# A third of the heads from head 10 on in key layout, exponentials kept in PSUM, in an LSH attention with a spatial gating MLP

## The chip, the cores and the metric

The program runs on one core of one Trainium2 chip. The metric is the device time of one execution in microseconds; of several executions, the median. A core has TensorE (PE; its weight loads are shown as PEld), VectorE (DVE), ScalarE (ACT), GpSimd (POOL) and the queue engine SyncE (SP), and sixteen DMA engines that all queues share.

## What is computed

Attention over 4 batches of 8 heads, 768 positions, head size 64, in which a query sees only the keys with the same 6-bit hash, followed by an MLP with a gate over positions. Cut to what matters:

```python
# q, k, v: (4, 8, 768, 64)
q_bits = (einsum('bhsd,dk->bhsk', q, proj) > 0)
k_bits = (einsum('bhsd,dk->bhsk', k, proj) > 0)
mask = q_bucket[:, :, :, None] == k_bucket[:, :, None, :]
scores = where(mask, scale * matmul(q, k.transpose(0, 1, 3, 2)), -1e9)
attn = exp(scores - max(scores, axis=-1))
attn = attn / (sum(attn, axis=-1) + 1e-09)
x = matmul(attn, v)                       # heads side by side: (4, 768, 512)

h = maximum(x @ w_in, 0.0)                # (4, 768, 1024)
u, w = h[..., :512], h[..., 512:]
w_n = (w - mean(w)) / sqrt(var(w) + 1e-06)
w_s = einsum('ts,bsd->btd', w_spatial, w_n) + b_spatial[None, :, None]
out = (u * w_s) @ w_out
```

## The kernel before

Numbers that need more than 16 bits are carried as two f16 tiles, a high and a low half, and a product of two such numbers takes three matmuls. The hash is folded into the score product: `ab[n % 4]` (four tiles in SBUF) holds queries, keys and hash rows of head n, so that scores and mask come out of four matmuls of 384 columns for each tile of 128 rows. There are 32 heads, n = 0 to 31, and 6 tiles each; two heads make a pair.

A head runs in one of two ways.

*Query layout* (`scores`, L278; `weighted`, L303). A tile has 128 queries in the partitions and 768 keys in the row. Four matmuls (L291, L292) fill a score buffer `sp`; VectorE finds the negated row maximum (L293, tile `jk`, value `nb`); ScalarE takes the exponential with that bias (L295) into an f32 tile `ex` in SBUF, of which there are three; ScalarE casts it to f16 as the high half of `pp` (L298); the low half is `ex` minus the high half (L299). That subtraction is on VectorE, but on GpSimd for tile 2 of the heads from 16 on, and for tiles 0 and 3 of the earlier ones (`PL_POOL`, `PL_POOL1`). Since the weighted sum needs keys in the partitions, a DMA turns `pp` into `pt` (L301, queue SP): 128 x 1536 f16. Then 18 matmuls (L314 to L316) add the tile to `pv`.

*Key layout* (`scores_k`, L256; `weighted_k`, L268), in heads 1 to 7, the set `KEYS`. A tile has 128 keys in the partitions, so that nothing has to be turned. But a row maximum over keys cannot be taken there, and it is found ahead: `row_max` (L235) makes two matmuls of 384 columns for each of six tiles (L241), a reduction on VectorE (L243), and after the sixth puts the maxima into a row of `ab` by way of a small transpose on PE and a transfer of `mt` on SP (L248 to L254). Scores then have the maximum subtracted already. The exponential (L265) goes to SBUF as f32, and six f32 matmuls (L275) weight `vf`, an f32 copy of v.

`normalize` (L318) divides `pv` by the row sums, `transpose_x` turns each pair's result by DMA (`xt`), and when a batch's four pairs are there its MLP is cut into 28 units (`mlp_units`: v, u, s and o), which are spread over the tiles of the next batch. The last batch's MLP runs after the last head. Weights are loaded, split and scaled in pieces during heads 0 to 12 (`weights_gen`).

*Buffers in PSUM.* The pool `ps_sc` has two score buffers of two banks each; `sp` of both layouts and the row maxima's `mp` take turns in them. Two banks are for `pv`, two for everything else. The pool is full.

*What sets the order.* The loop (L504) goes over g = 6 n + i. With `at(g, k)` each piece gets a due time: scores at g, the weighted sum of a query tile 5 tiles later (`LAG`), of a key tile 3 later (`LAGK`), the row maxima of head n from g = 6 n - 10 on, that is from the third tile of head n - 2. `build(n + 2)`, the loads of `ab`, is placed at tile 0 of head n, and after its transpose in SP's queue where head n is in query layout (L525). A scheduler then orders each engine's instructions by due time and by when it expects operands and buffers to be free; each engine executes its list strictly in order.

## Time and profile before

| | us |
|---|---|
| median of 3 runs | 736.97 |
| lowest, highest | 735.91, 740.86 |
| profiled execution, first to last instruction | 741.7 |
| one transpose of `pp`, time in SP's queue, median | 1.605 |
| score matmul of 384 columns (L291), mean | 0.344 |
| the 576 matmuls of the spatial product (L417), busy | 100.9 |

The profiled execution took 4.7 us more than the median of the runs. A group of matmuls overlaps itself: L417's 576 have a mean of 329 ns, but are busy for only 100.9 us together. Durations on PE are thus latencies, and the pace of a dense stretch is read from starts in the timeline. On the other engines an instruction's last 0.08 us or so can overlap the next one's start.

### The profile page before, as it was taken

The page shows a single profiled execution, that of the slowest core. Times are in us where ns is not written, and L with a number is a line of the kernel's source. Part 1 is how long each engine was busy: PE and PEld are TensorE (multiplying, and loading weights), DVE is VectorE, ACT ScalarE, POOL GpSimd, SP SyncE. Part 2 cuts the span into 40 slices and gives each one's busy share as a digit, 9 for nine tenths or more (in the row PEclk, how much of TensorE's full clock was granted, in tenths as well). Part 3 has the DMA queues.
Part 4 walks back from the last instruction along what each step waited for, and adds up shares of the span by engine and source line. Part 5 has one row for each costly group of instructions (what it writes and reads, how often), then busy time and mean ns, then how long its engine had stood idle before and what let it go on. Part 6 is the DMA issues. An engine that isn't in the chain of part 4 may idle for free.

```text
span 741.7 us, 14927 instructions
## 1 busy us (share of the span) xinstructions
PE 631.5 (85%) x5759; PEld 400.4 (54%) x5759; DVE 520.6 (70%) x945; ACT 434.8 (59%) x668; POOL 321.2 (43%) x324
## 2 busy tenths in 40 slices
PE   1569898998988776997898899889898998999997
PEld 0237686776445444554544555556455565654553
DVE  4677795536799999567689798678698987755200
ACT  1344574346788676655676577667677776743221
POOL 5122443123458675264314565156235571451503
PEclk9768797999999989898999999999999999999999
DMA  9565554324999989996999799999999999860011
GB/s 235 149 123 155 133 148 102 99 55 97 224 237 197 215 207 187 213 178 138 234 202 199 138 210 213 211 211 212 206 210 181 194 175 213 182 136 15 1 42 43
DMA packets 290011, 120.95 MB, mean 163 GB/s; under 512 B 270740, under 2 KB 273812, under 8 KB 289940
## 3 DMA queue, kind: packets, MB, share of 16 engines
q1 hardware_dynamic: 287636, 119.11, 76.4%
q10 hardware_dynamic: 2304, 0.89, 0.5%
q8 instruction: 45, 0.74, 0.4%
q14 instruction: 26, 0.21, 0.1%
HBM read 28.33 MB, written 6.29 MB: 47 GB/s over the span
## 4 chain that ended last, share of the span: by engine, by line
PE 43%; DMA 21%; DVE 13%; issue 8%; ACT 6%; POOL 6%; SPq 3%; ACTq 0%; DVEq 0%; POOLq 0%
DMA pt<-pp 14%; PE pv L275 6%; PE vps L361 6%; PE ops L432 5%; PE sps L417 5%; PE ups L402 5%; DMA ab<-hl 4%; PE sp L291 3%; DVE jk L293 3%; PE sp L292 3%; DVE pp L299 2%; PE sp L262 2%; PE pv L314 2%; ACT ex L295 2%; PE sp L263 2%
## 5 line engine op out<-in xcount | busy, mean ns | idle before, releaser
L295 ACT ACTIVATE ex<-sp,nb 128x768 f32<-128x768 f32 x150 | 134.1, 897 | 54.8 <-DVE jk L293 48.9
L299 DVE TENSOR_TENSOR pp<-ex,pp 128x768 f16<-128x768 f32 x116 | 126.2, 1089 | 47.6 <-ACT pp L298 46.5
L293 DVE TENSOR_SCALAR_CACHE_REDUCE jk<-sp 128x768 bf16<-128x768 f32 x150 | 142.4, 949 | 24.1 <-PE sp L292 22.2
L298 ACT CAST pp<-ex 128x768 f16<-128x768 f32 x150 | 124.3, 829 | 50.0 <-DMA pt<-pp 43.9
L314 PE MATMUL pv<-vp,pt 128*128 128x65 f16 x900 | 108.2, 198 | 40.5 <-DMA pt<-pp 40.2
L291 PE MATMUL sp<-ab 128*128 128x384 f16 x300 | 103.2, 344 | 31.6 <-ACT ex L295 19.3
L314 PEld LDWEIGHTS <-pt 128*128 128x128 f16 x900 | 86.7, 101 | 67.2 <-DMA pt<-pp 53.4
L299 POOL TENSOR_TENSOR pp<-ex,pp 128x768 f16<-128x768 f32 x34 | 58.1, 1708 | 131.1 <-ACT pp L298 124.6
L315 PE MATMUL pv<-vp,pt 128*128 128x64 f16 x900 | 108.0, 197 | 0.0
L316 PE MATMUL pv<-vp,pt 128*128 128x65 f16 x900 | 107.8, 198 | 0.0
L292 PE MATMUL sp<-ab 127*128 127x384 f16 x300 | 103.9, 346 | 0.0
L417 PE MATMUL sps<-ws,vn 128*128 128x384 f16 x576 | 100.9, 329 | 1.5 <-DVE sg L180 1.0
L315 PEld LDWEIGHTS <-pt 128*128 128x128 f16 x900 | 87.0, 100 | 11.3 <-issue 1.3
L316 PEld LDWEIGHTS <-pt 128*128 128x128 f16 x900 | 86.9, 100 | 3.1 <-issue 0.5
L417 PEld LDWEIGHTS <-vn 128*128 128x128 f16 x576 | 55.3, 99 | 37.8 <-issue 3.9
L432 PE MATMUL ops<-wo,g 128*128 128x512 f16 x288 | 70.9, 391 | 1.5 <-ACT o L436 0.9
L275 PEld LDWEIGHTS pv<-vf,ex 128*128 128x128 f32 x504 | 68.5, 208 | 4.1 <-issue 1.6
L402 PE MATMUL ups<-xt,wi 128*128 128x384 f16 x384 | 69.1, 333 | 1.3 <-ACT u L405 0.9
L361 PE MATMUL vps<-wi,xt 128*128 128x512 f16 x288 | 68.0, 383 | 1.4 <-DMA xt<-xs 1.3
L275 PE MATMUL pv<-vf,ex 128*128 128x65 f32 x504 | 67.0, 286 | 0.0
L333 POOL TENSOR_TENSOR x<-x,xf 128x384 f32<-128x384 f32 x32 | 35.5, 1110 | 64.1 <-DVE x L332 64.1
L422 POOL TENSOR_TENSOR sy<-sy,u 128x384 f32<-128x384 f32 x32 | 36.6, 1145 | 49.3 <-DVE sy L421 49.2
(87 smaller groups left out, 1010.7 us busy)
## 6 DMA issues: line engine op xcount, KB each, us to landing
qk<-kq SPq DMA_DIRECT2D x16, 768.0 KB
ab<-hl SPq DMA_DIRECT2D x31, 384.0 KB
ab<-hl SPq DMA_DIRECT2D x34, 192.0 KB
out<-o SPq DMA_DIRECT2D x24, 256.0 KB
v<-v SPq DMA_DIRECT2D x13, 384.0 KB
raw<-w_in SPq DMA_DIRECT2D x16, 256.0 KB
pt<-pp SPq DMA_TRANSPOSE x150
raw<-w_sp SPq DMA_DIRECT2D x12, 192.0 KB
```

Of the source, the lines that this page charges most:

```text
L275: nc.tensor.matmul(acc[:, qi, :], lhsT=ex[:, qi * P:(qi + 1) * P], rhs=vf[p % 2][:, 2 * i + e, :], start=(i == 0 and qi == 0), stop=(i == ...
L291: nc.tensor.matmul(ps[:, c], lhsT=t[:, 0, qs], rhs=t[:, 1, cs], start=True, stop=False)
L292: nc.tensor.matmul(ps[:, c], lhsT=t[0:P - 1, 3, qs], rhs=t[0:P - 1, 2, cs], start=False, stop=True)
L293: nc.vector.tensor_scalar(jk, ps, -ISQ, None, op0=ALU.mult, op1=ALU.min, accum_out=nb)
L295: st["ex", n, i] = nc.scalar.activation(ex, ps, AF.Exp, bias=nb, scale=ISQ).ins
L298: nc.scalar.copy(pp[:, 0], ex)
L299: (nc.gpsimd if i in (PL_POOL if n >= 2 * NH else PL_POOL1) else nc.vector).tensor_tensor(out=pp[:, 1], in0=ex, in1=pp[:, 0], op=ALU.subtract)
L314: nc.tensor.matmul(acc, lhsT=pt[:, c, :], rhs=vh, start=(i == 0 and c == 0), stop=False)
L315: nc.tensor.matmul(acc[:, 0:D], lhsT=pt[:, c, :], rhs=vl, start=False, stop=False)
L316: nc.tensor.matmul(acc, lhsT=pt[:, NT + c, :], rhs=vh, start=False, stop=(i == NT - 1 and c == NT - 1))
L361: nc.tensor.matmul(ps, lhsT=xt[c][:, gx, i * P:(i + 1) * P], rhs=wi[gw][:, c, F2:DF], start=(k == 0), stop=(k == 3 * NPAIR - 1))
L417: nc.tensor.matmul(ps[:, :HS], lhsT=vn[gv][:, c, d * P:(d + 1) * P], rhs=ws[gw][:, c, hs], start=(k == 0), stop=(k == 3 * NT - 1))
```

## The change

`KEYS` becomes two sets: `KF32`, heads 1 to 7 as before, and `KSPLIT`, heads 10, 13, 16, 19, 22, 25, 28 and 31, which change from query to key layout. Their scores and row maxima are those of the other key heads. Their exponential is written back into its score buffer in PSUM, ScalarE copies it as f16 into the high half of a tile `pk` in SBUF (L267 of the new kernel), and VectorE subtracts that from the PSUM tile into the low half (L268). The weighted sum takes 18 f16 matmuls with the split v, as a query tile's. `pk` takes a buffer of the tag `pt`.

Heads in query layout change too: the exponential stays in the score buffer (L310), cast and subtraction read it there (L313, L314), and every subtraction is on VectorE. The three `ex` tiles in SBUF are gone, and so are the tables of tiles for GpSimd.

```diff
+        if n in KSPLIT:
+            pp = wk.tile([P, 2, 2, HS], F16, tag="pt", bufs=PTB, name=f"pk{n}_{i}")
+            st["ex", n, i] = nc.scalar.activation(ps, ps, AF.Exp, scale=ISQ).ins
+            nc.scalar.copy(pp[:, 0], ps)
+            nc.vector.tensor_tensor(out=pp[:, 1], in0=ps, in1=pp[:, 0], op=ALU.subtract)
+            st["pt", n, i] = pp
+            return
...
+        if n in KSPLIT:
+            pk = ex.rearrange("p g c q -> p g (c q)")
+            vl, vh = vp[p % 2][:, 2 * i + e, 0:D], vp[p % 2][:, 2 * i + e, D:2 * D + 1]
+            for qi in range(NT):
+                qs = slice(qi * P, (qi + 1) * P)
+                nc.tensor.matmul(acc[:, qi, :], lhsT=pk[:, 0, qs], rhs=vh, start=(i == 0 and qi == 0), stop=False)
+                nc.tensor.matmul(acc[:, qi, 0:D], lhsT=pk[:, 0, qs], rhs=vl, start=False, stop=False)
+                nc.tensor.matmul(acc[:, qi, :], lhsT=pk[:, 1, qs], rhs=vh, start=False, stop=(i == NT - 1 and qi == NT - 1))
+            return
...
-        ex = wk.tile([P, 2, HS], F32, tag="ex", bufs=EB, name=f"ex{n}_{i}")
-        st["ex", n, i] = nc.scalar.activation(ex, ps, AF.Exp, bias=nb, scale=ISQ).ins
+        st["ex", n, i] = nc.scalar.activation(ps, ps, AF.Exp, bias=nb, scale=ISQ).ins
         at(NT * n + i + G_H, 50)
         pp = wk.tile([P, 2, 2, HS], F16, tag="pp", bufs=PB, name=f"pp{n}_{i}")
-        nc.scalar.copy(pp[:, 0], ex)
-        (nc.gpsimd if i in (PL_POOL if n >= 2 * NH else PL_POOL1) else nc.vector).tensor_tensor(out=pp[:, 1], in0=ex, in1=pp[:, 0], op=ALU.subtract)
+        nc.scalar.copy(pp[:, 0], ps)
+        nc.vector.tensor_tensor(out=pp[:, 1], in0=ps, in1=pp[:, 0], op=ALU.subtract)
...
-    PL_POOL = (2,)
-    KEYS = {1, 2, 3, 4, 5, 6, 7}
-    PL_POOL1 = (0,3)
+    KF32 = {1, 2, 3, 4, 5, 6, 7}
+    KSPLIT = {10, 13, 16, 19, 22, 25, 28, 31}
+    KEYS = KF32 | KSPLIT
...
-    EB = 3
```

`has_keys`, `has_queries` and the scale in `normalize` ask `KF32` in place of `KEYS`.

The scheduler makes new orders of this. Names in the rows: `jk20_3` is the minimum of tile 3 of head 20, `pp20_3` the low half's subtraction, `sp` the score buffer, `mx22` a row maximum of head 22 read from `mp22_0` and so on, `rv`, `x`, `xs` are `normalize`, `vp` the split v, `sy` the MLP's spatial unit.

VectorE's list in head 20, before:

```order
L299 TENSOR_TENSOR pp20_1_5250<-ex20_1_5248,pp20_1_5250 128x768
L293 TENSOR_SCALAR jk20_3_5329,nb20_5178<-sp20_3_5330 128x768
L328 TENSOR_SCALAR rv19_5421<-pv19_5159 128x6
L329 RECIPROCAL rv19_5421<-rv19_5421 128x6
L330 SCALAR_TENSOR_TENSOR rv19_5421<-nb19_4893,rv19_5421 128x6
L332 TENSOR_TENSOR x19_5425<-pv19_5159,rv19_5421 128x384
L421 SCALAR_TENSOR_TENSOR sy1_2_0_5324<-sps1_2_0_5305,bt_108 128x384
L299 TENSOR_TENSOR pp20_3_5338<-ex20_3_5336,pp20_3_5338 128x768
L293 TENSOR_SCALAR jk20_4_5385,nb20_5178<-sp20_4_5386 128x768
L339 TENSOR_TENSOR xs9_5114<-x19_5425,xs9_5114 128x6x64
L293 TENSOR_SCALAR jk20_5_5432,nb20_5178<-sp20_5_5433 128x768
L299 TENSOR_TENSOR pp20_4_5394<-ex20_4_5392,pp20_4_5394 128x768
```

The same place after:

```order
L314 TENSOR_TENSOR pp20_2_5273<-sp20_2_5266,pp20_2_5273 128x768
L243 TENSOR_REDUCE mx22_5278<-mp22_0_5279 128x1
L309 TENSOR_SCALAR jk20_3_5340,nb20_5172<-sp20_3_5341 128x768
L243 TENSOR_REDUCE mx22_5278<-mp22_1_5353 128x1
L309 TENSOR_SCALAR jk20_4_5381,nb20_5172<-sp20_4_5382 128x768
L314 TENSOR_TENSOR pp20_3_5348<-sp20_3_5341,pp20_3_5348 128x768
L243 TENSOR_REDUCE mx22_5278<-mp22_2_5394 128x1
L314 TENSOR_TENSOR pp20_4_5389<-sp20_4_5382,pp20_4_5389 128x768
L309 TENSOR_SCALAR jk20_5_5398,nb20_5172<-sp20_5_5399 128x768
L243 TENSOR_REDUCE mx22_5278<-mp22_3_5411 128x1
L219 SCALAR_TENSOR_TENSOR vp1_95<-v32_11_4924,vp1_95 128x12x64
L314 TENSOR_TENSOR pp20_5_5406<-sp20_5_5399,pp20_5_5406 128x768
```

The subtraction of 20_2 has come from GpSimd, each one reads `sp`, and the row maxima of head 22 stand between the tiles of head 20; the minimum of 20_3 now stands behind the subtraction of 20_2, and that of 20_5 behind the one of 20_4.

On TensorE, in the same place after, the row-maximum matmuls of mp22_0 and the twelve matmuls of an output unit (`ops`) stand between the scores of 20_2 and those of 20_3; from there on one `mp22` follows each tile's scores.

SP's queue from the end of head 21 to the beginning of head 23, before:

```order
L301 DMA_TRANSPOSE pt21_5_5747<-pp21_5_5744 128x12x128
L152 DMA qk13_5749<-kq 128x1536
L301 DMA_TRANSPOSE pt22_0_5783<-pp22_0_5780 128x12x128
L211 DMA ab0_82<-hl12_5636 64x2x1536
L212 DMA ab0_82<-hl12_5636 64x1536
L301 DMA_TRANSPOSE pt22_1_5835<-pp22_1_5832 128x12x128
L301 DMA_TRANSPOSE pt22_2_5867<-pp22_2_5864 128x12x128
L301 DMA_TRANSPOSE pt22_3_5913<-pp22_3_5910 128x12x128
L301 DMA_TRANSPOSE pt22_4_5959<-pp22_4_5956 128x12x128
L344 DMA_TRANSPOSE xt10_5992<-xs10_5717 128x12x128
L301 DMA_TRANSPOSE pt22_5_6006<-pp22_5_6003 128x12x128
L301 DMA_TRANSPOSE pt23_0_6077<-pp23_0_6074 128x12x128
```

And after:

```order
L316 DMA_TRANSPOSE pt21_5_5727<-pp21_5_5724 128x12x128
L152 DMA qk13_5729<-kq 128x1536
L359 DMA_TRANSPOSE xt10_5946<-xs10_5698 128x12x128
L316 DMA_TRANSPOSE pt23_0_6061<-pp23_0_6058 128x12x128
L211 DMA ab1_83<-hl12_5618 64x2x1536
L212 DMA ab1_83<-hl12_5618 64x1536
L316 DMA_TRANSPOSE pt23_1_6098<-pp23_1_6095 128x12x128
```

The six transposes of head 22 are gone, and the loads of ab0 that stood among them are issued earlier, during head 21.

More of the change, by code (lines that the diff above doesn't have):

```diff
@@ L165, in has_keys @@
     def has_keys(p):
-        return 2 * p in KEYS or 2 * p + 1 in KEYS
+        return 2 * p in KF32 or 2 * p + 1 in KF32
     def has_queries(p):
-        return not (2 * p in KEYS and 2 * p + 1 in KEYS)
+        return not (2 * p in KF32 and 2 * p + 1 in KF32)
     def hash_rows(p):
@@ L327, in normalize @@
         rv = wk.tile([P, NT], F32, tag="rv", bufs=2, name=f"rv{n}")
-        nc.vector.tensor_scalar(rv, pv[:, :, D], 1e-9, 1.0 / SX if n in KEYS else SQ / SX, op0=ALU.add, op1=ALU.mult)
+        nc.vector.tensor_scalar(rv, pv[:, :, D], 1e-9, 1.0 / SX if n in KF32 else SQ / SX, op0=ALU.add, op1=ALU.mult)
         nc.vector.reciprocal(rv, rv)
```

## The prediction

> **What bounds the kernel now.** I read the page first, for the shares and the DMA row, then stretches cut where the attention's stages change, then the waits, then the groups by line, and last the timeline of one undisturbed tile. The page: busy time of each engine, and the slices with the granted TensorE clock and the DMA share.
>
> ```profile
> PE 631.5 (85%) x5759; PEld 400.4 (54%) x5759; DVE 520.6 (70%) x945; ACT 434.8 (59%) x668; POOL 321.2 (43%) x324
> PEclk9768797999999989898999999999999999999999
> DMA  9565554324999989996999799999999999860011
> ```
>
> No engine is full over the span, but the DMA row stands at 9 from slice 10 to 33, which is heads 8 to 31. The stretches (us; busy time of PE, PEld, DVE, ACT, POOL; clock; DMA share; GB/s) are batch 0's heads 1 to 7, heads 8 to 15, heads 16 to 30, and head 31 with the last MLP; the last row is VectorE's work at L293 alone, the negated row minimum that each query tile has once.
>
> ```profile
> 62.00:172.00 110.00, 102.36 (x738) 82.34 (x736) 71.86 (x151) 57.96 (x102) 36.22 (x50) 0.91 0.41 106
> 172.00:348.00 176.00, 142.23 (x1402) 87.44 (x1402) 147.08 (x252) 122.41 (x197) 99.97 (x91) 0.92 0.96 197
> 348.00:637.00 289.00, 257.13 (x2718) 158.32 (x2717) 232.74 (x427) 200.38 (x289) 130.15 (x120) 0.97 1.00 199
> 637.00:741.70 104.70, 99.88 (x714) 56.26 (x711) 33.66 (x67) 34.47 (x61) 36.91 (x36) 0.99 0.26 62
> ...
> 348.00:637.00 289.00, 86.16 (x180) 0.97 1.00 199
> ```
>
> The 180 records of the last row are 90 tiles (each has a second, short one), so 15 heads in 289 us: 19.3 us a head, 57.8 for three. Heads 8 to 15 take 176 / 8 = 22.0 each, 66 for three. From 348 on the DMA share is 1.00, so DMA sets 19.3 us a head; PE has 257.1 / 15 = 17.1, DVE 15.5, ACT 13.4. What one transpose weighs shows where little else is moved: the DMA queue's issues and the share of the same stretch.
>
> ```profile
> 638.12 2.46 SPq L344 DMA_TRANSPOSE xt<-xs  x1
> 640.69 16.48 SPq L301 DMA_TRANSPOSE pt<-pp  x7
> ...
> 637.00:660.00 23.00, 22.86 (x289) 15.62 (x287) 16.46 (x28) 13.23 (x19) 13.43 (x13) 1.00 0.83 160
> ```
>
> With one that was issued just before and lands here that is nine transposes in 23 x 0.83 = 19.1 us: 2.1 us of all sixteen engines each. A head has six, and half of one of xt: 13.7 of its 19.3 us. The waits of the whole span (us in total, times, longest) say the same, and show a second limit in its beginnings.
>
> ```profile
> PEld L314 <- DMA pt<-pp: 53.4, 37, 4.1
> ACT pp L298 <- DMA pt<-pp: 43.9, 33, 3.7
> PE sp L291 <- ACT ex L295: 19.3, 16, 5.1
> ```
>
> The first two are the transposes: their result is late, and the tile pp that one reads comes free late. The third is TensorE waiting until an exponential has emptied one of the two score buffers (ps_sc) in PSUM.
>
> **The change part by part.** The durations that I use, by group (count | busy us, mean ns of one | idle before):
>
> ```profile
> L293 DVE TENSOR_SCALAR_CACHE_REDUCE jk<-sp 128x768 bf16<-128x768 f32 x150 | 142.4, 949 | 24.1 <-PE sp L292 22.2
> L295 ACT ACTIVATE ex<-sp,nb 128x768 f32<-128x768 f32 x150 | 134.1, 897 | 54.8 <-DVE jk L293 48.9
> L299 DVE TENSOR_TENSOR pp<-ex,pp 128x768 f16<-128x768 f32 x116 | 126.2, 1089 | 47.6 <-ACT pp L298 46.5
> L298 ACT CAST pp<-ex 128x768 f16<-128x768 f32 x150 | 124.3, 829 | 50.0 <-DMA pt<-pp 43.9
> L299 POOL TENSOR_TENSOR pp<-ex,pp 128x768 f16<-128x768 f32 x34 | 58.1, 1708 | 131.1 <-ACT pp L298 124.6
> ...
> L243 DVE TENSOR_REDUCE mx<-mp 128x1 f32<-128x768 f32 x42 | 39.8, 952 | 23.3 <-PE mp L241 23.2
> L265 ACT ACTIVATE ex<-sp 128x768 f32<-128x768 f32 x42 | 33.9, 806 | 32.2 <-PE sp L263 28.9 <-PE mp L241 3.0
> ...
> L339 DVE TENSOR_TENSOR xs<-x,xs 128x384 f16<-128x384 f32 x32 | 20.1, 628 | 3.7 <-ACT xs L338 3.7
> L421 DVE SCALAR_TENSOR_TENSOR sy<-sps,bt 128x384 f32<-128x384 f32 x32 | 17.6, 551 | 39.9 <-PE sps L417 39.9
> ```
>
> *Transposes.* Eight heads lose six each: 48 x 2.1 = 101 us of DMA time and their places in SP's queue. Three heads then need 57.8 - 6 x 2.1 = 45.2 us of DMA, so DMA stops being the bound. Nothing is gained unless what is late next is earlier than 57.8.
>
> *Row maxima.* 48 tiles more of L241 to L243: two 384-wide matmuls, 0.163 us apart in the timeline below, so 2.0 us of PE for three heads, and a reduction of 0.952 on DVE, against which the same heads lose 48 of L293's 0.949. Eight small transfers of mt join SP's queue; each waits there for DVE's copy into mt, with transposes queued behind it, so it costs at most a fraction of the slack that DMA has gained. PE then needs 51.4 + 2.0 = 53.4 us for three heads.
>
> *Low halves.* The 34 subtractions on POOL (1.708) go to DVE, and all 150 read the exponential from PSUM. No row shows this form. The nearest: at 384 elements sy, with one operand in PSUM, takes 551 ns, xs, with both in SBUF, 628; and an undisturbed subtraction of before takes 0.96 (below). I take 0.95, with ends of 0.88 and 1.09. DVE for three heads is 46.5, and three POOL tiles come for 2.7 while the others save about 0.1 each: 47 to 48, not the bound. In heads 8 to 15, where DVE is busy for 147 of 176 us, 16 tiles come from POOL: 14 us more, less 3 saved.
>
> The Trainium skill, page "Perfetto Trace Analysis", section "Optimizing Scalar/DVE Operations", speaks against this step: it gives VectorE a fixed overhead of about 60 ns on SBUF and 125 on PSUM, and ScalarE 93 and 51. The pair of rows above goes the other way for VectorE. By the page the subtraction would be 65 ns dearer and the copy 42 cheaper, an estimate of 96 x 0.023 = 2 us more on the chains of the query tiles.
>
> *Exponentials into PSUM.* No row shows ScalarE writing PSUM; 0.81 (L265, no bias) and 0.90 (L295) bound it, and I keep 0.90 for query tiles, 0.81 for key tiles. ACT, at 13.4 of 19.3 us, has room for either.
>
> *How long a score buffer is held.* This is the term that decides. Before, a tile gives its buffer back when the exponential ends; after, when the subtraction ends. What waits then is PE, at the next tile's score matmuls, and behind them in its order stand weighted matmuls and MLP units that are ready. One tile of head 31 that hardly waits, start and duration in us, PE's first and last score matmul, and two weighted ones for their pace:
>
> ```profile
> 636.71 0.33 PE L291 MATMUL sp<-ab 128*128 128x384 f16 x1
> ...
> 637.20 0.33 PE L292 MATMUL sp<-ab 127*128 127x384 f16 x1
> 637.37 0.19 PE L314 MATMUL pv<-vp,pt 128*128 128x65 f16 x1
> 637.40 0.19 PE L315 MATMUL pv<-vp,pt 128*128 128x64 f16 x1
> ...
> 637.57 0.96 DVE L293 TENSOR_SCALAR_CACHE_REDUCE jk<-sp 128x768 bf16<-128x768 f32 x1 [0.52 <-PE sp L292]
> ...
> 638.57 0.90 ACT L295 ACTIVATE ex<-sp,nb 128x768 f32<-128x768 f32 x1 [0.66 <-DVE jk L293]
> 639.50 0.83 ACT L298 CAST pp<-ex 128x768 f16<-128x768 f32 x1
> ...
> 640.36 0.96 DVE L299 TENSOR_TENSOR pp<-ex,pp 128x768 f16<-128x768 f32 x1
> ```
>
> Held from 636.71 to 639.47 before: 2.76 us; to 641.32 after: 4.6. A split key tile needs 0.82 + 0.81 + 0.83 + 0.95 with hops: 3.5; a row maximum 0.5 + 0.95: 1.4 to 1.5. Three heads need 12 x 4.6 + 6 x 3.5 + 6 x 1.45 = 85 us of buffer, 42 of two buffers, if nothing ever waits. But DVE, ACT and PE take their work in a fixed order. The order shown above has, on DVE, the next tile's minimum behind the last subtraction for most tiles (55 of 88 from head 8 on; before, 14 of 111), and a row maximum in the other buffer meanwhile.
>
> So I walked heads 20 to 22 by hand through the orders of PE, DVE and ACT: each instruction starts when its engine is done with the one before, its operands are there and its buffer is free, with the durations above (weighted matmuls 0.03 apart, 384-wide ones 0.163, 512-wide 0.216, the small DVE operations of normalize 0.9 in all). The minimum of 20_0 starts at 0, its subtraction ends at 4.95. Tile 20_1 has the minimum at 2.9 and ends at 7.8; 20_2 at 5.9 and 9.95. Then mp22_0 and twelve output matmuls (2.6) stand on PE before the scores of 20_3: 12.2 and 16.85. 20_4: 15.0 and 19.35. 20_5 waits behind a row maximum in the buffer of 20_3: 19.45 and 24.1. Head 21 ends its subtractions at 28.7, 31.4, 35.9, 39.9, 44.7 and 46.7, the key tiles of head 22 at 48.3, 53.3, 54.9, 58.4, 60.4 and 63.2; the minimum of 23_0 starts at 64.3. This is 64.3 us for three heads against 57.8, and in these heads PE's own work is light (44 us; heads 17 to 19 have 60, the mean is 52). I take 66 as the mean.
>
> *Sum, against the profiled 741.7.* Heads 16 to 30, five threes: 5 x (66 - 57.8) = +41. Heads 8 to 15: 8 / 3 x (66 - 66) = 0, and 11 us more on DVE, of which half lies in waits: +5. Heads 0 to 7: head 0 alone changes, six longer holds beside the row maxima of heads 1 and 2, +2 (0 to 10). The end (104.7 us, PE busy for 99.9): head 31 needs no transposes, and PE's order has 26 spatial matmuls (4 us) fewer behind its first tile: -5. Total +43: 784.7. The median of the runs is 4.7 below the profiled span, so 780.
>
> **The rivals.** *Faster: the order fits, and DMA relief is what counts.* Row maxima and normalize fill the gaps in which ACT works, and PE is late next: 53.4 to 55 us for three heads. Then heads 16 to 30 give 5 x 3.6 = 18, heads 8 to 15 perhaps 17, the end 5: 697 to 705. For it speaks that 99 us of waits on pt vanish by a third; against it the walk, which finds the buffers late even with nothing else late. It decides if three heads stay under 57.
>
> *The change is hidden:* the holds take back what DMA gives, three heads at 57 to 59: 730 to 745.
>
> *Slower still: the row maximum waits for its operands.* The key head's ab is loaded from the first tile of the head two before, and mp22_0 stands on PE ahead of the scores of 20_3. The chain shows how long such a load takes there:
>
> ```profile
> 289.54 6.07 DMA ab<-hl
> 457.37 4.74 DMA ab<-hl
> ```
>
> It is issued behind the transpose of 20_0, at about 6.5 in the walk, and lands at 11 to 13; mp22_0 is due at 7.9. PE would stand for 4 us, once in each of eight threes: 780 + 32 = 812.
>
> **How the numbers follow.** Longer holds as walked 0.48 (780, own range 757 to 800); with the late operands 0.21 (812); hidden 0.11; faster 0.20 (700). A measurement of this kernel tells about 1% from no change. Faster by over 1% is below 729.6: 0.20; within 1%: 0.10; slower: 0.70. The range 720 to 825 leaves out most of the faster case (0.14) and what lies above 825 (0.05).
>
> **What would show it.** In the profile of after: DMA share well below 1.00 between heads 16 and 30, no large ACT wait on pt; PE's wait at the score matmuls (L307, L266's tiles) on the subtraction L314 and L268, far over 19.3 us, in place of waits on pt; threes of heads at 62 to 70 us; L314 on DVE at 0.95. Wrong would be: threes under 57 us with PE over 92% busy (the faster rival), or a DVE subtraction from PSUM above 1.1, or PE's wait at L241 on DMA (the late operands).

## The result and the profile after

| | us |
|---|---|
| before, median (range) | 736.4 (733.9 to 740.9) |
| after, median (range) | 851.9 (847.5 to 857.5) |
| ratio, 95% interval | 1.157 (1.150 to 1.164) |
| profiled execution before, after | 741.7, 845.7 |

The changed kernel is slower by 115 us, where +43 was forecast, and the time lies above the range. The profiled execution after is the fastest of its four runs and the one before the slowest of its four, so the two profiles are only 104 us apart. The page of the kernel after, busy time of each engine and two rows of slices (granted TensorE clock, DMA share):

```profile
PE 686.7 (81%) x5863; PEld 420.8 (50%) x5863; DVE 515.0 (61%) x947; ACT 430.9 (51%) x668; POOL 231.4 (27%) x298
...
PEclk9859698987999599799969867996997999899999
DMA  8667362265756782775585369448716826611010
```

The plateau of nines in the DMA row is gone, and no engine has taken its place: VectorE and GpSimd are idler than before. TensorE is busy for 55 us more, though the change gives it only 96 more matmuls of 384 columns and eight small transposes. The stretches of the kernel after, cut at the first score matmul of heads 1, 8, 16 and 31 (columns as before: us; busy time of PE, PEld, DVE, ACT, POOL; clock; DMA share; GB/s):

```profile
52.00:174.60 122.60, 109.83 (x799) 87.32 (x798) 74.50 (x159) 60.10 (x106) 35.73 (x52) 0.88 0.46 110
174.60:380.50 205.90, 160.72 (x1466) 94.59 (x1465) 144.49 (x269) 121.90 (x196) 64.10 (x80) 0.86 0.66 146
380.50:741.20 360.70, 295.50 (x2810) 174.85 (x2809) 237.37 (x421) 198.21 (x288) 86.78 (x107) 0.87 0.60 127
741.20:845.70 104.50, 96.70 (x661) 53.19 (x656) 26.79 (x56) 33.80 (x61) 32.66 (x35) 0.98 0.11 35
```

Heads 16 to 30 took 291.2 us before, between the same marks, and take 360.7 now: 72.1 for three heads. The DMA share fell from 1.00 to 0.60, so the transposes bind no more, and yet everything is later. The clock column fell from 0.97 to 0.87. Heads 8 to 15 went from 172.5 to 205.9. The rest hardly moved: up to head 8 +1.6, the end -0.6.

The groups of the kernel after that are new or changed (count | busy us, mean ns | idle before):

```profile
L309 DVE TENSOR_SCALAR_CACHE_REDUCE jk<-sp 128x768 bf16<-128x768 f32 x102 | 97.1, 952 | 58.0 <-PE sp L308 54.9 <-PE pv L331 1.6 <-PE pv L288 0.8
L314 DVE TENSOR_TENSOR pp<-sp,pp 128x768 f16<-128x768 f32 x102 | 97.0, 951 | 25.7 <-ACT pp L313 25.3
L310 ACT ACTIVATE sp<-sp,nb 128x768 f32<-128x768 f32 x102 | 89.2, 874 | 132.9 <-DVE jk L309 128.9 <-DMA ab<-sg 1.9 <-DVE rv L343 0.8
...
L313 ACT CAST pp<-sp 128x768 f16<-128x768 f32 x102 | 81.3, 798 | 11.1 <-DMA ab<-sg 5.5 <-ACT sp L310 3.8
L268 DVE TENSOR_TENSOR pk<-sp,pk 128x768 f16<-128x768 f32 x48 | 45.5, 952 | 35.1 <-ACT pk L267 34.8
L266 ACT ACTIVATE sp<-sp 128x768 f32<-128x768 f32 x48 | 38.3, 798 | 16.0 <-PE sp L263 14.6 <-DVE sy L436 1.1
```

No operation in these rows is dearer than it was costed. What these two engines lost stands in the idle columns: ScalarE waits for the row minimum, and VectorE's row minimum for scores. Waits of the kernel after (us in total, times, longest):

```profile
PEld L329 <- DMA pt<-pp: 56.9, 53, 3.8
DVE jk L309 <- PE sp L308: 54.9, 49, 3.9
...
PE sp L307 <- DVE mx L243: 32.4, 34, 1.8
...
PE mp L241 <- DVE pp L314: 25.2, 15, 3.6
...
PE mp L241 <- DMA ab<-hl: 5.8, 4, 1.7
...
PE sp L307 <- DVE pp L314: 4.8, 4, 1.5
...
PE sp L262 <- DVE pk L268: 4.5, 7, 1.2
```

The third row was 2.0 us before, and the fourth is new: scores waiting for the buffer that a row maximum has, and row maxima waiting for the buffer that a subtraction still reads. The row maxima and the score tiles block each other in the two buffers. The wait that the prediction named as its sign, of score matmuls on a subtraction, is small: the last two rows and 3.1 us of L307 on L268, 12.4 in all.

### The profile page after: what moved, and what is told of

Its sections match the earlier page's. It is cut to its first block, busy times and chain, and to the rows that moved or that the text cites. A ratio compares the mean times of both kernels' runs of the same rounds, so it can differ in the third digit from the quotient of the medians.

```text
span 845.7 us, 14952 instructions
## 1 busy us (share of the span) xinstructions
PE 686.7 (81%) x5863; PEld 420.8 (50%) x5863; DVE 515.0 (61%) x947; ACT 430.9 (51%) x668; POOL 231.4 (27%) x298
## 4 chain that ended last, share of the span: by engine, by line
PE 49%; DMA 18%; DVE 15%; issue 6%; ACT 6%; POOL 2%; SPq 2%; ACTq 0%; DVEq 0%; POOLq 0%
DMA pt<-pp 11%; PE sps L432 9%; PE ups L417 5%; PE ops L447 5%; PE vps L376 5%; PE pv L291 4%; DMA ab<-hl 4%; DVE mx L243 4%; PE sp L307 3%; PE sp L308 3%; PE mp L241 3%; DVE pp L314 3%; DVE jk L309 3%; PE sp L262 2%; PE sp L263 2%
## 5 line engine op out<-in xcount | busy, mean ns | idle before, releaser
L310 ACT ACTIVATE sp<-sp,nb 128x768 f32<-128x768 f32 x102 | 89.2, 874 | 132.9 <-DVE jk L309 128.9
L309 DVE TENSOR_SCALAR_CACHE_REDUCE jk<-sp 128x768 bf16<-128x768 f32 x102 | 97.1, 952 | 58.0 <-PE sp L308 54.9
L307 PE MATMUL sp<-ab 128*128 128x384 f16 x204 | 79.3, 389 | 49.2 <-DVE mx L243 32.4
L243 DVE TENSOR_REDUCE mx<-mp 128x1 f32<-128x768 f32 x90 | 85.6, 952 | 50.6 <-PE mp L241 49.9
L329 PE MATMUL pv<-vp,pt 128*128 128x65 f16 x612 | 84.5, 208 | 34.9 <-DMA pt<-pp 34.6
L314 DVE TENSOR_TENSOR pp<-sp,pp 128x768 f16<-128x768 f32 x102 | 97.0, 951 | 25.7 <-ACT pp L313 25.3
L329 PEld LDWEIGHTS <-pt 128*128 128x128 f16 x612 | 63.5, 107 | 62.4 <-DMA pt<-pp 56.9
L241 PE MATMUL mp<-ab 127*128 127x384 f16 x180 | 58.1, 414 | 36.3 <-DVE pp L314 25.2
L313 ACT CAST pp<-sp 128x768 f16<-128x768 f32 x102 | 81.3, 798 | 11.1 <-DMA ab<-sg 5.5
L331 PE MATMUL pv<-vp,pt 128*128 128x65 f16 x612 | 85.0, 209 | 0.0
L348 POOL TENSOR_TENSOR x<-x,xf 128x384 f32<-128x384 f32 x32 | 32.4, 1014 | 156.7 <-DVE x L347 141.6
L262 PE MATMUL sp<-ab 128*128 128x384 f16 x180 | 61.6, 343 | 9.5 <-DVE pk L268 4.5
L330 PEld LDWEIGHTS <-pt 128*128 128x128 f16 x612 | 64.3, 108 | 5.9 <-issue 1.9
L268 DVE TENSOR_TENSOR pk<-sp,pk 128x768 f16<-128x768 f32 x48 | 45.5, 952 | 35.1 <-ACT pk L267 34.8
```

The source lines that it names most:

```text
L243: nc.vector.reduce_max(st["mx", n][:, i:i + 1], ps, axis=AX.XY)
L307: nc.tensor.matmul(ps[:, c], lhsT=t[:, 0, qs], rhs=t[:, 1, cs], start=True, stop=False)
L309: nc.vector.tensor_scalar(jk, ps, -ISQ, None, op0=ALU.mult, op1=ALU.min, accum_out=nb)
L314: nc.vector.tensor_tensor(out=pp[:, 1], in0=ps, in1=pp[:, 0], op=ALU.subtract)
L329: nc.tensor.matmul(acc, lhsT=pt[:, c, :], rhs=vh, start=(i == 0 and c == 0), stop=False)
L330: nc.tensor.matmul(acc[:, 0:D], lhsT=pt[:, c, :], rhs=vl, start=False, stop=False)
```

## Where head 20 loses its time

The walk of the prediction went through heads 20 to 22, so its first head is looked at closely. TensorE in the kernel after (start, duration, line, operation); the rows left out are the other matmuls of the same groups:

```profile
480.67 0.50 PE L307 MATMUL sp<-ab 128*128 128x384 f16 x1 [1.52 <-DVE pp L314]
...
481.61 0.53 PE L308 MATMUL sp<-ab 127*128 127x384 f16 x1
483.90 0.23 PE L329 MATMUL pv<-vp,pt 128*128 128x65 f16 x1 [1.77 <-DMA pt<-pp]
...
486.34 0.82 PE L241 MATMUL mp<-ab 127*128 127x384 f16 x2 [1.28 <-DMA ab<-hl]
486.96 0.63 PE L230 MATMUL mp<-vc,ones 128*128 128x128 f32 x2
487.38 4.01 PE L447 MATMUL ops<-wo,g 128*128 128x512 f16 x12
491.23 0.33 PE L307 MATMUL sp<-ab 128*128 128x384 f16 x1
...
491.72 0.33 PE L308 MATMUL sp<-ab 127*128 127x384 f16 x1
```

From the scores of tile 20_2 (480.67) to those of 20_3 (491.23) pass 10.6 us. Between them stands the first row maximum of head 22, which waits for its `ab`. SP's queue in the same kernel shows when that load was issued:

```profile
480.68 1.42 SPq L316 DMA_TRANSPOSE pt<-pp  x1
482.14 0.69 SPq L211 DMA_DIRECT2D ab<-hl  x1
482.88 0.58 SPq L212 DMA_DIRECT2D ab<-hl  x1
```

It stands behind the transpose of 20_0, and the row maximum that needs it starts 3.5 us after the second issue. When the two score buffers came free is seen on VectorE, at the ends of the subtractions of 20_1 and 20_2:

```profile
483.05 0.95 DVE L314 TENSOR_TENSOR pp<-sp,pp 128x768 f16<-128x768 f32 x1
...
485.20 0.96 DVE L314 TENSOR_TENSOR pp<-sp,pp 128x768 f16<-128x768 f32 x1
```

One buffer was free at 484.00, the other at 486.16. The scores of 20_3 did not get the first, though their due time is the earlier one: the loop asks for a buffer for `mp22_0` before it asks for one for 20_3, and TensorE's order follows the asking (read from the program and the orders, not tried by itself). So the free buffer stood until `ab` had landed, and behind the row maximum the order has the twelve output matmuls, another 3.85 us.

And the four score matmuls of 20_2 start 0.31 us apart, where 20_3's start 0.163 apart: TensorE ran at half its clock, as the stretches there show (us; PE busy; clock; DMA share; GB/s):

```profile
478.00:482.00 4.00, 2.48 (x24) 0.71 0.07 15
482.00:486.00 4.00, 1.29 (x19) 0.50 1.03 208
486.00:490.00 4.00, 3.66 (x11) 0.51 1.34 167
490.00:494.00 4.00, 3.49 (x50) 1.00 0.92 229
```

How the clock falls and comes back shows in stretches of 4 us some 60 us earlier (columns as before):

```profile
416.00:420.00 4.00, 2.06 (x12) 1.00 0.00 0
420.00:424.00 4.00, 1.14 (x18) 0.71 0.43 98
424.00:428.00 4.00, 2.89 (x25) 0.50 0.89 153
428.00:432.00 4.00, 2.07 (x15) 0.50 0.46 97
432.00:436.00 4.00, 2.95 (x18) 0.50 0.88 225
436.00:440.00 4.00, 3.70 (x24) 0.66 1.13 236
440.00:444.00 4.00, 4.00 (x39) 1.00 1.16 164
```

TensorE is idle for 4.8 of 8 us, the clock falls to 0.50, and it comes back only once TensorE has been nearly full for some 4 us. Cut into stretches of 2 us, 74 of the 361 us of heads 16 to 30 have a clock of 0.54 or less, against 12 of 291 before.

The Trainium skill, page "TensorE: Matmul & The Clock Gate", section "Part 1: The HAM clock gate", says that the clock is halved after an idle window of about 3.4 us and restored after about as long a busy one. The rows above agree, with 0.50 and 1.00 at both ends, except that the window before the fall need not be wholly idle: by the trace TensorE was busy for 0.5 of the 3.4 us before the clock fell, at 421.6, and stood for 0.3 of the 5 us before it came back, at 438.7. The walk, which took full clock throughout, had left this out.

## The experiments

All times are medians of the device time. The kernel before ran beside each and gave 735.7 to 741.5 us in the five sets of runs, so a difference of under 5 us between kernels of different sets tells nothing. Stage lengths below are cut as above. "Holds" stands for: exponential, cast and subtraction all in the score buffer.

### The parts of the change alone

**Key layout alone.** The changed kernel with every exponential in SBUF again and the low halves as before on VectorE and GpSimd:

```diff
-            st["ex", n, i] = nc.scalar.activation(ps, ps, AF.Exp, scale=ISQ).ins
-            nc.scalar.copy(pp[:, 0], ps)
-            nc.vector.tensor_tensor(out=pp[:, 1], in0=ps, in1=pp[:, 0], op=ALU.subtract)
+            ex = wk.tile([P, 2, HS], F32, tag="ex", bufs=EB, name=f"ex{n}_{i}")
+            st["ex", n, i] = nc.scalar.activation(ex, ps, AF.Exp, scale=ISQ).ins
+            nc.scalar.copy(pp[:, 0], ex)
+            nc.vector.tensor_tensor(out=pp[:, 1], in0=ex, in1=pp[:, 0], op=ALU.subtract)
...
-        st["ex", n, i] = nc.scalar.activation(ps, ps, AF.Exp, bias=nb, scale=ISQ).ins
+        ex = wk.tile([P, 2, HS], F32, tag="ex", bufs=EB, name=f"ex{n}_{i}")
+        st["ex", n, i] = nc.scalar.activation(ex, ps, AF.Exp, bias=nb, scale=ISQ).ins
```

> The changed kernel with every exponential in an f32 tile in SBUF again (three tiles, shared by query and split key tiles) and the low halves back on GpSimd for the tiles that had it there; the eight split key heads stay. Theory H (the loss is the longer hold of the two score buffers): the 115 us vanish and DMA relief shows, 700 to 745 us. Theory K (the loss is the key layout itself: 48 row maxima more in the order of PE and VectorE): 810 to 850. Theory B (only both together cost): 735 to 780.

788.9 us (787.7 to 791.6), ratio 1.071 (1.062 to 1.080). Key layout costs 52 us by itself, though it takes 48 transposes from the DMA engines.

**Holds alone.** The changed kernel with no head changed to key layout:

```diff
-    KSPLIT = {10, 13, 16, 19, 22, 25, 28, 31}
+    KSPLIT = set()
```

> The changed kernel without split key heads: heads 8 to 31 all in query layout, exponentials in PSUM, all low halves on VectorE. Theory H: slow, 790 to 850 us, with DMA share under 0.9 between heads 16 and 30 and PE waiting at the score matmuls on the subtraction. Theory K: within 2% of before, 735 to 750. Theory B: 745 to 780.

828.5 us (825.6 to 834.4), ratio 1.126 (1.116 to 1.136): +92. Its heads 16 to 30:

```profile
365.10:721.60 356.50, 295.13 (x2807) 174.82 (x2808) 239.34 (x445) 203.37 (x293) 90.40 (x110) 0.88 0.78 163
```

All 48 transposes are still there, and the DMA share is down to 0.78 because the stage has become 65 us longer. Here the wait that the prediction named does show, over the whole span:

```profile
PE sp L307 <- DVE pp L314: 30.5, 25, 3.5
```

**Holds in key tiles only.** The changed kernel with the query tiles' exponentials in SBUF, all low halves on VectorE as in the changed kernel:

```diff
-        st["ex", n, i] = nc.scalar.activation(ps, ps, AF.Exp, bias=nb, scale=ISQ).ins
+        ex = wk.tile([P, 2, HS], F32, tag="ex", bufs=EB, name=f"ex{n}_{i}")
+        st["ex", n, i] = nc.scalar.activation(ex, ps, AF.Exp, bias=nb, scale=ISQ).ins
```

> The changed kernel with the query tiles' exponentials in SBUF, all low halves on VectorE; only the 48 split key tiles hold their buffer to the subtraction (3.5 us at least, where a query tile before held 2.8). Theory H: the query tiles carry the loss, so within 25 us of the kernel with all exponentials in SBUF. Theory K: 810 to 850.

798.0 us (793.5 to 798.3), ratio 1.082 (1.074 to 1.090): 54 less than the changed kernel, 9 more than key layout alone. Of the holds, the query tiles' are what costs.

**All subtractions on VectorE, nothing else.** The kernel before without its tables for GpSimd:

```diff
-        (nc.gpsimd if i in (PL_POOL if n >= 2 * NH else PL_POOL1) else nc.vector).tensor_tensor(out=pp[:, 1], in0=ex, in1=pp[:, 0], op=ALU.subtract)
+        nc.vector.tensor_tensor(out=pp[:, 1], in0=ex, in1=pp[:, 0], op=ALU.subtract)
```

> Before with one part alone: the 34 low halves of GpSimd on VectorE, exponentials in SBUF, no split key heads. VectorE gets some 30 us of work, 11 of them in heads 8 to 15 where it is busy for 147 of 176 us. If VectorE's load mattered: 745 to 760 us. If DMA hides it, as it does from head 16 on: 732 to 745.

735.1 us, ratio 0.999 (0.995 to 1.002): no difference. The move from GpSimd is not a cost.

So 52 and 92 by themselves stand beside 115 together, which is less than their sum. Both use the same two buffers.

### What the row maxima cost

Key layout should have gained by the transposes. So its row maxima were added where nothing needs them, and taken away where they stand. First, the kernel before with the row maxima of the eight heads found, and not used:

```diff
-    rml = [(NT * n + i - NT - LEAD, n, i) for n in sorted(KEYS) for i in range(NT)]
+    rml = [(NT * n + i - NT - LEAD, n, i) for n in sorted(KEYS | EXTRA) for i in range(NT)]
```

> The kernel before, in which heads 10, 13, 16 and so on to 31 stay in query layout, but their row maxima are found ahead as well (48 tiles of row_max, eight small transposes and transfers) and never used. If the row maxima, by their turns in the two score buffers, are what key layout costs (+52 us with every exponential in SBUF), this kernel loses 40 to 60 us: 776 to 796. If what costs is the changed order of the weighted sums and of the MLP units, it loses only the work itself, at most 15 us: 737 to 752.

806.7 us (800.0 to 809.1), ratio 1.089 (1.083 to 1.094): +66, more than either theory gave. Then the kernel with key layout alone, the row maxima of the eight heads left out (a stale row is subtracted, `nb` is zero):

```diff
-    rml = [(NT * n + i - NT - LEAD, n, i) for n in sorted(KEYS) for i in range(NT)]
+    rml = [(NT * n + i - NT - LEAD, n, i) for n in sorted(KF32) for i in range(NT)]
```

> The eight heads in key layout with every exponential in SBUF (788.9 us with row maxima), but their row maxima are left out: nothing is found ahead, their scores have a stale row subtracted. If the row maxima are the cost, this kernel lies at or below the one before, since a third of the transposes is gone: 700 to 740 us. If the order or the key heads themselves are the cost, it stays at 770 us or above.

710.2 us (708.3 to 713.4), ratio 0.960 (0.956 to 0.964). Here is what the faster rival had hoped for: without row maxima and holds the transposes saved are worth 26 us (30 against the kernel before that ran beside it), and heads 16 to 30 run close to TensorE:

```profile
328.70:603.10 274.40, 253.34 (x2757) 157.13 (x2754) 214.85 (x378) 198.62 (x290) 122.80 (x120) 0.98 0.79 167
```

That is 54.9 us for three heads, PE busy for 92% of it at a clock of 0.98. The row maxima take it back: 710 to 789, +79 us for 48 tiles. The same with the holds (the changed kernel, row maxima of the eight heads left out by the same edit):

> The changed kernel without the row maxima of the eight heads (their scores have a stale row subtracted). If the long holds and the row maxima are short of the same two buffers, the holds alone still cost most of what they cost without key layout (+92 us against its own base): against the 710 us of the kernel with no holds and no row maxima, 770 to 800. If the holds only cost because a row maximum stands in the other buffer, it falls to 710 to 740.

790.5 us (787.3 to 794.4). The holds cost 80 us with no row maximum near them, so they don't need one in the other buffer to hurt. Beside them the row maxima cost 61 us (851.9 - 790.5), not 79.

### Turns, operand or work

**Row maxima through other banks.** Instead of a score buffer, each row maximum takes two single banks of the MLP units' pool, with two reductions of 384 columns. Once in the kernel with key layout alone, once in the kernel before with unused row maxima:

```diff
-        ps = ps_sc.tile([P, 2, 512], F32, tag="sc", name=f"mp{n}_{i}")[:, :, :HS]
         for c in range(2):
-            nc.tensor.matmul(ps[:, c], lhsT=t[0:P - 1, 3, i * P:(i + 1) * P],
+            ps = ps_m.tile([P, 512], F32, tag=MT, name=f"mp{n}_{i}_{c}")[:, :HS]
+            nc.tensor.matmul(ps, lhsT=t[0:P - 1, 3, i * P:(i + 1) * P],
                              rhs=t[0:P - 1, 2, c * HS:(c + 1) * HS], start=True, stop=True)
-        nc.vector.reduce_max(st["mx", n][:, i:i + 1], ps, axis=AX.XY)
+            nc.vector.reduce_max(st["mx", n][:, i, c:c + 1], ps, axis=AX.X)
```

> Key layout for the eight heads with every exponential in SBUF (788.9 us), but all row maxima go through the two single banks of the MLP units instead of the score buffers: two reductions of 384 columns for each tile and a small maximum for each head, so VectorE works more than before (about 0.2 us a tile, 8 us in heads 16 to 30). If it is the row maxima's turns in the score buffers that cost 52 us, this kernel comes near the one without row maxima (710 us): 715 to 750. If it is their work on VectorE and TensorE and their place in the order, it stays at 775 us or above. In between (750 to 775), the MLP's two banks have become what is short.

> The kernel before with the row maxima of the eight heads found and not used (806.7 us), these again through the MLP units' banks. Turns in the score buffers: back to 740 to 765 us. Work and order: 790 us or above.

813.7 us (811.1 to 814.5), 25 more than through the score buffers, and 796.2 (793.1 to 802.0). The second is hardly less than the 806.7 through the score buffers: the kernel before ran 5 us faster beside it, and the ratios are 1.084 and 1.089. Neither falls to the times that buffer turns alone would give. The edit moves the turn rather than removing it: the MLP units now take turns with the row maxima, and the time goes from the head two before to the key head itself (head 22 takes 28.5 us in the first of these kernels, 16.3 with the score buffers). The two runs don't decide; the next do.

**The operand later or earlier.** In the kernel with key layout alone TensorE shows the same stop as in head 20 above, filled with MLP work that the order has put there:

```profile
452.30 6.01 PE L434 MATMUL sps<-ws,vn 128*128 128x384 f16 x36
...
459.21 0.34 PE L241 MATMUL mp<-ab 127*128 127x384 f16 x1 [0.80 <-DMA ab<-hl]
459.38 0.33 PE L308 MATMUL sp<-ab 128*128 128x384 f16 x1
```

and SP's queue its load:

```profile
453.53 1.41 SPq L318 DMA_TRANSPOSE pt<-pp  x1
455.00 0.68 SPq L211 DMA_DIRECT2D ab<-hl  x1
455.73 0.59 SPq L212 DMA_DIRECT2D ab<-hl  x1
```

The scores of 20_2 began at 451.1; those of 20_3 follow 8.3 us later. In three kernels the row maxima were made due three tiles later (`EXTRA` in place of `KSPLIT` in the third):

```diff
-    rml = [(NT * n + i - NT - LEAD, n, i) for n in sorted(KEYS) for i in range(NT)]
+    rml = [(NT * n + i - NT - (1 if n in KSPLIT else LEAD), n, i) for n in sorted(KEYS) for i in range(NT)]
```

and in a fourth, the kernel with key layout alone, the load was let out from behind the transpose:

```diff
-            if n not in KEYS:
+            if n not in KEYS and not (i == BI and n + 2 in KSPLIT):
                 stack.enter_context(tc.issue_after(st["tr"]))
```

> Key layout for the eight heads, exponentials in SBUF (788.9 us), with their row maxima due three tiles later: from tile 5 of the head two before, not from tile 2. Theory of the late operand: the first row maximum needs ab, which is loaded in that same head behind the transpose of its first tile, and the scores of the next tiles stand behind it in the turn of the score buffers; three tiles later ab is there, so most of the 52 us goes: 725 to 755, and the long heads (26 to 30 us) are gone. Theory of buffer turns and VectorE work: nothing is saved by coming later, 775 us or above.

> The changed kernel (851.9 us) with the row maxima of the eight heads due three tiles later. Late operand: it comes near the changed kernel without row maxima (790 us): 785 to 820. Buffer turns and VectorE work: 840 us or above.

> The kernel before with the eight heads' row maxima found and not used (806.7 us), due three tiles later. Late operand: 740 to 770. Buffer turns and VectorE work: 790 us or above.

> Key layout for the eight heads, exponentials in SBUF (788.9 us), row maxima due where they were, but the eight loads of ab that they need no longer placed behind the transpose of the first tile in the queue of SP. Late operand: the load is issued some 7 us earlier and the scores of tile 3 follow those of tile 2 without the stop of 8 to 14 us; 735 to 765. Buffer turns and VectorE work: within 1% of 788.9.

Key layout alone: 773.6 us (767.6 to 776.6) with later row maxima, 771.0 (767.9 to 772.3) with the earlier load; the kernel before with unused row maxima: 791.5 (785.3 to 795.5); the changed kernel: 865.5 (862.7 to 867.6), 14 more than without the edit. The earlier load did what it should, as TensorE in that kernel shows:

```profile
437.31 3.57 PE L434 MATMUL sps<-ws,vn 128*128 128x384 f16 x21
440.72 0.49 PE L241 MATMUL mp<-ab 127*128 127x384 f16 x2
441.05 1.79 PE L434 MATMUL sps<-ws,vn 128*128 128x384 f16 x10
442.67 0.33 PE L308 MATMUL sp<-ab 128*128 128x384 f16 x1
```

No wait for `ab` is left, but the scores of 20_3 still come 6.6 us after those of 20_2 (436.10). So the late operand is real and worth 15 to 20 us of the 79 (15 and 18 by the medians, 18 and 19 by the ratios to the kernel before), not most of it. Where the holds bind as well, later row maxima gained nothing; the earlier load was not tried there.

**The reduction.** The kernel with key layout alone, in which the eight heads' row maxima keep matmuls, loads and turns, but VectorE reads 16 columns (the result is multiplied by zero):

```diff
-        nc.vector.reduce_max(st["mx", n][:, i:i + 1], ps, axis=AX.XY)
+        nc.vector.reduce_max(st["mx", n][:, i:i + 1], ps[:, :, 0:8] if n in KSPLIT else ps, axis=AX.XY)
```

and the kernel without row maxima, to which 48 reductions of a constant in SBUF are added at the same due times:

```diff
+        if n in KSPLIT:
+            nc.vector.reduce_max(st["mx", n][:, i:i + 1], bt.rearrange("p (c q) -> p c q", c=2), axis=AX.XY)
+            return
```

> Key layout, exponentials in SBUF (788.9 us). The eight heads' row maxima keep their matmuls, their loads, their turns in the score buffers and their small transpose, but the reduction on VectorE reads 16 of the 768 columns and its result is multiplied by zero, so no maximum is subtracted. If VectorE's reduction (0.95 us a tile, and the hold of the buffer that comes with it) is the cost, this falls by 35 us or more, to 755 or below. If the turn in the buffers and the late operand are, it stays at 770 to 789.

> The kernel without row maxima for the eight heads (710.2 us), to which 48 reductions of 768 columns on VectorE are added at the same due times, read from a constant in SBUF: VectorE's work alone, no matmul, no score buffer, no operand to wait for. If VectorE's work is the cost: 745 us or above. If the turns and the operand are: 705 to 728.

759.4 us (756.8 to 761.8) and 731.4 (728.5 to 738.6). The groups of the reductions, in the first and in the second kernel:

```profile
L243 DVE TENSOR_REDUCE mx<-mp 128x1 f32<-128x16 f32 (+1 forms) x90 | 47.9, 534 | 40.2 <-PE mp L241 40.0
```

```profile
L240 DVE TENSOR_REDUCE mx<-bt 128x1 f32<-128x768 f32 x48 | 41.9, 930 | 0.0
```

The first row mixes 42 long reductions (0.95 us) with 48 short ones of (47.9 - 42 x 0.95) / 48 = 0.17. Cutting them saves 30 of the 79 us; 41.9 us of reductions added alone cost 21. Both results lie between the theories: VectorE's work is 21 to 30 us, where the 30 also hold that a score buffer comes free sooner after a short reduction; and what remains, 759 - 710 = 49, is matmuls, turns and the operand together.

### A third score buffer

The changed kernel, the kernel before and the kernel with key layout alone, each with three score buffers, the two banks taken from the weighted sums and from the MLP units:

```diff
-    PSB = (2,2,2)
+    PSB = (3,1,1)
```

> The changed kernel with three score buffers in PSUM instead of two; the two banks come from the pools of the weighted sums and of the MLP units, which keep one each. To be read against the kernel before with the same pools, run beside it. If the two score buffers are what the change is short of, the distance between the two drops from 115 us to under 40 us. If the fixed order on VectorE and TensorE sets the pace whatever the buffers are, the distance stays over 80 us. The stage of heads 16 to 30 then shows waits of the score matmuls on the subtraction near zero in the first case.

> The kernel before with three score buffers and one bank each for weighted sums and MLP units: the price of the missing banks. It is bound by transposes, so a third score buffer can gain little: 735 to 800 us, all of what is over 736 being the single banks. Both theories expect the same here; it is the base for the run beside it.

> Key layout for the eight heads, exponentials in SBUF, three score buffers, one bank each for the weighted sums and the MLP units. Against the changed kernel with three buffers (763.0 us) only the holds go. If three buffers leave the holds covered, 750 to 765 us; if the holds still bind with three, 720 to 745 us.

763.0 us (758.8 to 767.7), 802.0 (795.4 to 806.9) and 803.0 (798.0 to 809.0). The distance between the changed kernel and the one before went from +115 to -39, which is what a shortage of buffers would do: heads 16 to 30 of the changed kernel take 293.4 us with three buffers, 360.7 with two. But the third run fits no theory: with three buffers the kernel without holds is 40 us slower than the one with them. Its heads 16 to 30 take 315.9 us against 293.4, its end 138.9 against 128.8. Two places in each key head carry more than the difference. From the score tile behind which the first row maximum starts to the next tile pass 14.1 us on average, against 6.5 with the holds, and from the key head's first score tile to its second 9.7 against 1.9. The two kernels differ in where the low halves are made, too, and each has an order of its own; which of these it is stays open.

### What one tile costs

The runs come together in one number, worked out from the starts of the score matmuls on TensorE in each trace: the mean time from a tile's first score matmul to the next tile's, over the 143 intervals from the first tile of head 8 to the last of head 31. They are sorted by the tile that begins them, and by whether a row maximum starts inside.

| kernel | query tile, none inside | query tile, a row maximum inside | key tile |
|---|---|---|---|
| before | 3.33 (143) | | |
| holds alone | 3.91 (143) | | |
| key layout alone | 2.96 (48) | 5.25 (48) | 2.83 (47) |
| after | 3.86 (48) | 5.10 (48) | 3.29 (47) |
| no row maxima, no holds | 3.10 (96) | | 3.12 (47) |
| no row maxima, holds | 3.88 (96) | | 3.21 (47) |
| before, row maxima unused | 2.93 (95) | 5.43 (48) | |
| key layout, earlier load | 3.15 (48) | 4.62 (48) | 2.78 (47) |
| key layout, short reduction | 2.89 (48) | 4.54 (48) | 2.96 (47) |
| after, three score buffers | 3.22 (48) | 4.39 (48) | 2.52 (47) |

An interval with a row maximum inside is 2.3 us longer than one without (5.25 against 2.96, with key layout alone). The first row maximum of each key head has the largest part: its intervals take 8.6 us, those of the five others 3.5 to 6.2. The earlier load brings it to 6.2, and 8 x 2.4 = 19 us is about all that this load saved; the short reduction leaves it at 8.6. From before to key layout alone: 48 x (5.25 - 3.33) - 48 x 0.37 - 47 x 0.50 = +51, which are the 52 us measured. From there to after: 48 x 0.90 + 47 x 0.46 - 48 x 0.15 = +58 of 63. And the last sum says why the two parts don't add: the holds lengthen only the intervals in which no row maximum stands.

No kernel that computes the whole of the reference beat the one before by over 1%.

## Why the prediction was wrong

*Right:* slower; the price of each operation (subtraction from PSUM 0.951 for 0.95, exponential into PSUM 0.874 and 0.798 for 0.90 and 0.81); the DMA engines stop binding (0.60); GpSimd's share costs nothing where DMA bound; heads 0 to 7 (+1.6 for +2). The sentence of the Trainium skill weighed there (page "Perfetto Trace Analysis", section "Optimizing Scalar/DVE Operations") was right in sign for ScalarE, whose copy from PSUM took 798 ns against 829, and not for VectorE, whose subtraction took 951 against the undisturbed 0.96 us.

*The step that failed* is "I take 66 as the mean" for three heads. It measured 72.1, so heads 16 to 30 gave +70 for +41. Heads 20 to 22, walked to 64.3, took 74.6. The walk was wrong in its fourth tile already: it put the minimum of 20_3 at 12.2 after that of 20_0, and it came at 16.3. The rows of head 20 give the reasons. The walk started `mp22_0` at its due place, 7.9; it started at 486.34 - 475.77 = 10.6, when its `ab` had landed: 2.7 us. Not all of that is the load's, since TensorE had stood for 1.8 us before, until the transposed 20_0 was there, and then done 18 weighted matmuls at half clock; for `ab` alone it stood 1.3 us. And twelve output matmuls costed at 2.6 us took 3.8 (487.38 to 491.23), with the clock at 0.51 for most of them: 1.2 us. Together 3.9 of the 4.1. The walk had every operand there in time and the clock full; where the other 6 of the 10 us that it missed in three heads went was not followed.

The term for the row maxima fell short in the same way: 2.0 us of TensorE for three heads and an even exchange on VectorE, with their turns and waits left to the walk. They measured 79 us without the holds and 61 with them.

*The rival that was split off* held the first of these: "The row maximum waits for its operands", with the load at 6.5 (it was issued 6.4 after) landing at 11 to 13. It was priced at 32 us as another case, when it belongs into every case; even so it would have given 812, not 852. The sign that it was to be known by misled as well: TensorE's wait at L241 on DMA is only 5.8 us in the whole span, because an order that expects the load to be late puts other work ahead of it, and it is the next scores that come late. Its weight, as tried, is 15 to 20 us without holds; with them, later row maxima won nothing back.

*The second failed step* is "Heads 8 to 15: 8 / 3 x (66 - 66) = 0", and 5 us for VectorE. They gave +33, so that the profiles differ by +70 +33 +1.6 -0.6 = 104 where +43 was forecast. That these heads took 22 us each before didn't mean that their score tiles had 66 us for three to spare: holds alone make them 16 us longer (188.5), key layout alone 21.5 (194.0), and without row maxima and holds they fall to 156.7.

*The end* was forecast at -5 and came out at -0.6; no run looked into it. *The sign* named for the holds, score matmuls waiting for the subtraction, came to 12.4 us after and 30.5 with holds alone; with row maxima between, it is the row maximum that waits for the subtraction (25.2 us) and the scores that wait for the row maximum (32.4). In the faster rival the 99 us of waits on `pt` are 97 by the rows shown (53.4 + 43.9), which changes nothing.

*How far the half clock carries the rest* was not tried by itself. Busy time of TensorE in heads 16 to 30 rose from 259.3 (the same marks) to 295.5 us, of which 60 row-maximum matmuls at 0.163 us are 10. The other 26 us are an upper end for what the clock can have taken there directly. The mean clock of that stage was 0.87 after, 0.88 with holds alone, 0.94 with key layout alone, 0.95 with holds and no row maxima, and 0.98 with neither. The two lowest belong to the two kernels in which TensorE is idle for the largest part of the stage (18 and 17%), the highest to the one with the least (8%); the two between, idle for 13 and 15%, stand the other way round.

What is shown: row maxima cost 79 us without the holds and 61 with them; of the 79, tried one at a time, 21 to 30 are the reduction and 15 to 20 the late operand. Holds cost 63 us beside the row maxima, 80 without them, and 92 where no head is in key layout. The saved transposes are worth 26 to 30. Not shown: how the remaining 30 to 40 us of the row maxima split between matmuls and turns, and by which wait the holds act. A third buffer takes the changed kernel from 852 to 763, which speaks for the buffers, but the run with key layout alone and three of them contradicts it.

## What to carry to other kernels

When a saved resource is the bound, price the thing that pays for it by what stands between two uses of the scarcest buffer, not by its busy time: here 48 row maxima, whose reductions take 0.95 us each, cost 79 us, because each put an operand, a turn and a reduction between two score tiles. Causes that act on the same turn are walked together in one forecast, not listed as rivals. And a wait that the order has been planned around shows on no engine as a wait: look at the gap between two successive uses of the buffer instead.

## What the hardware showed beyond that

- The granted clock fell to 0.50 within 8 us in which TensorE was busy for 3.2, and came back after some 5 us of nearly full work; score matmuls under the half clock started 0.31 us apart (20_2), not 0.163 (20_3). A wait of a few us so makes the work behind it slower, too.
- ScalarE was no slower for writing its exponential into the PSUM buffer that it reads (874 ns, against 897 into SBUF), and VectorE's subtraction cost the same from PSUM as from SBUF when undisturbed (951 ns against 0.96 us; over whole kernels the mean from SBUF was higher, 1089 ns before and 1053 with all of them on VectorE).
